# Four interleaved attention layers in one kernel: the second sliding layer's products in four column groups and its layer norms spread over the products; in the last layer, the next block's operands loaded a quad ahead and left-over projections carried on

## The chip, the cores and the metric

The kernel runs on one core of one Trainium2 chip. The metric is device time in microseconds (us), the median of several runs. The core's engines appear as in the profile: PE is TensorE (matmuls; its weight loads are listed as PEld), DVE is VectorE, ACT is ScalarE, POOL is GpSimd, SP is SyncE, on which nearly all DMAs are issued, one after the other in program order.

## What is computed

Input x is 2048 x 512 (one batch). Four layers follow each other; layers 0 and 2 use the weights A and a sliding window of 256 keys, layers 1 and 3 the weights B and all keys. Each layer is a layer norm, a projection to q, k and v of 32 heads of 16, softmax attention, a projection, and the residual.

```
def _A_ref(x, wqkv, wo):            # H = 32 heads, Dh = 16, W = 256
    q, k, v = split heads of x @ wqkv
    scores = einsum("bhqd,bhkd->bhqk", q, k) * Dh**-0.5
    mask = (i - j >= 0) & (i - j < W)
    p = softmax(where(mask, scores, -1e9))
    return heads joined of einsum("bhqk,bhkd->bhqd", p, v) @ wo
def _B_ref(...)                     # the same without the mask
x = A_x
x = x + _A_ref(_layernorm(x), A_wqkv, A_wo)    # layer 0
x = x + _B_ref(_layernorm(x), B_wqkv, B_wo)    # layer 1
x = x + _A_ref(_layernorm(x), A_wqkv, A_wo)    # layer 2
x = x + _B_ref(_layernorm(x), B_wqkv, B_wo)    # layer 3
```

## The kernel before

**Tiles.** The 2048 rows are four blocks c of 512 rows, each four tiles i of 128 rows. The 32 heads are eight quads qd of four heads. One attention step makes the scores of a quad for some keys on PE (`exps`, L745; products of 64 rows by 128 columns of the array), their exponentials on ACT (L749), and two steps later the product with v on PE (L799 in full layers, L833 in sliding ones; four groups of 32 columns, one per head; a column of ones in v gives the row sums). In a sliding layer a quad has three steps, and POOL masks the edges of each (L822, L825). In a full layer it has 16 steps. `epilogue` (L690 to L735) turns a quad's result on DVE (`ot`), divides it by the row sums and splits it into two half-precision terms (`oh`).

**Layers and loops.** Layers 0, 1 and 2 run over c and, inside, over the eight quads. Layer 3 runs over t (four pairs of quads), then c, then the two quads of t, 16 steps each. In the text steps are counted through the program: layer 1 has the steps 176 to 687, layer 3 the steps 864 to 1375. A step of a sliding layer makes two counts, so layer 2, whose block 0 has less to do, has the counts 688 to 863 in 88 steps.

**The other work** (projections K, Q, V of the next layer, the output projection `wo`, norms, transposes) is a list of `Work` generators beside the attention. `mms` (L383) issues one product as 12 matmuls (3 in O3). `PH["full"]` says that a full layer is running: then each matmul is issued as four matmuls of 32 columns (L395), otherwise as one of 128 (L398). `Side` decides after every step how much of the list goes in: `step` for sliding layers, `share` with a budget per step (its lowest value is `least`) for full ones. `finish` (L989), at the end of every block, issues all that is left of the block's list at once, apart from weight preparations.

**A layer norm.** `wo` (L659) finishes a tile of x with DVE (L672), stores it, and after the fourth tile calls `norm` (L427), which issues at once a reciprocal root of a dozen small DVE instructions and for each of the four tiles `xn` and `xh` (L448) and their difference (L454). A work T then calls `transposed` (L475) for the four tiles: a DMA transpose on SP from `xh` to `xc`, the operand of the next projections. A product with `xc` as the moving operand needs all four tiles of the block.

**Layer 3** makes the keys and queries of the next pair t+1 (K3, Q3), their maximum products (`hsum`, L562) and shifts (the store `qs<-m`, L597), the upper half of v, and the part of the output projection `wo_part` (O3) of each finished block. Blocks load their quads with `load_full` (L760 for q, L770 for k), one quad ahead inside a block, and at a block's start for its first quad.

Of the kernel before, what the change touches and what calls it, by code (L numbers as in the profile page):

```python
# [15 lines left out]
ALU = mybir.AluOpType  # L16
# [3 lines left out]
P = 128  # L20
# [169 lines left out]
def fast_path(ctx, tc, flag, a_x, a_wqkv, a_wo, b_wqkv, b_wo, out):  # L190
# [23 lines left out]
    clock, DONE, XNR, ONR = [0.0], {}, {}, {}  # L214
    LAST, STORES, EARLY = {}, [], {}

# [165 lines left out]

    def mms(ps, pairs, after=1.6, us=MM, go=True):  # L383


        if PH["full"] and pend:
            settle()
            PH["free"] = clock[0] + 1.6
            yield 0.1
        if PH["win"]:  # L390
            PH["unit"], PH["extra"] = PH["now"], 0
        for i, (a, b) in enumerate(pairs):
            if PH["full"]:
                for g in range(0, P, 32):
                    nc.tensor.matmul(ps[g:g + 32], a[:, g:g + 32], b, start=(i == 0), stop=(i == len(pairs) - 1),  # L395
                                     skip_group_check=True)
            else:
                nc.tensor.matmul(ps, a, b, start=(go and i == 0), stop=(i == len(pairs) - 1))  # L398
# [21 lines left out]
    def norm(l, c, xs, tail=False):  # L420
# [4 lines left out]
        return out  # L425

    def norm_tiles(l, c, xs, out, tail=False):  # L427

        mv = ST[l, c][1]
        y = rsqrt(nc, vp, f"{l}_{c}", mv[:, :, 1])  # L430
        if tail:
# [13 lines left out]
        for i in range(4):  # L445
            xn = vp.tile([P, D], F32, name=f"xn{l}_{c}_{i}", tag="xn", bufs=1)
            xh = vp.tile([P, 2, D], F16, name=f"xh{l}_{c}_{i}", tag="xh", bufs=XNB)
            norm1 = lambda o: nc.vector.tensor_scalar(o, xs[i], mv[:, i, 0:1], y[:, i:i + 1], op0=ALU.subtract, op1=ALU.mult)  # L448
            norm1(xn)
            if tail:  # L450
                nc.scalar.activation(xh[:, 0], xs[i], AF.Identity, bias=nb[:, i:i + 1], scale=y[:, i:i + 1])
            else:
                norm1(xh[:, 0])
            nc.vector.tensor_tensor(xh[:, 1], xn, xh[:, 0], ALU.subtract)  # L454
# [40 lines left out]

    def transpose(l, c, xns):
        for i, xh in enumerate(xns):
            yield "wait", XNR[l, c] + 2.3 * i
            transposed(l, c, i, xh)
# [159 lines left out]
    def wo(l, c, tail):  # L659

        w = weights(l % 2, 3, f"o{l}_{c}")
        xs = load_x(l, c) if tail else None
        yield wait(8)
        if not tail:
# [176 lines left out]
    class Work:  # L841
# [37 lines left out]

        done = begun = open = going = False  # L880
        proj = property(lambda self: self.name is not None and self.name[0] in ("K", "Q", "K3", "Q3"))
# [27 lines left out]
    class Side:  # L909
# [99 lines left out]
    def attention(l, works):  # L1009
# [5 lines left out]
        for t in range(NHT if l == 3 else 1):  # L1015
            for c in range(NQ):
                qds = range(2 * t, 2 * t + 2) if l == 3 else range(NQD)
                PH["spare"] = (3, 3, 2, 0)[c] if l == 2 else 0
                if l == 1:

                    sd = sd or Side(NT * NQD // 2, works[0], works[1], 0.33)
                    while ("Q", 1, c) not in DONE:
                        sd.one(True)
                    settle()
                else:
                    sd = Side((3 if win else NT) * len(qds), works[t * NQ + c], works[t * NQ + c + 1], 0.28 if l == 3 and t < 3 else 0.0)
                if win:
                    PH["run"] = RUN
                ops = loaded.pop((c, qds[0]), None) or load(l, c, qds[0])
                for qd in qds:  # L1030
                    if (l, c, qd) == (1, 0, NQD // 2):
                        sd.finish()
                        sd = Side(NT * NQD * NQ - NT * NQD // 2, works[1], works[2], 0.33)
                    nxt = None
                    if qd + 1 in qds:
                        nxt = load(l, c, qd + 1)
                    elif l < 3 and c + 1 < NQ and ("Q", l, c + 1) in DONE and (l == 1 or ("K", l, c + 1) in DONE):
                        if any(f == ("Q", l, c + 1) for _, _, f in pend):
# [4 lines left out]
                    for f in (attn_win if win else attn_full)(l, c, qd, *ops, a):  # L1043
# [4 lines left out]
                        if (l, t, c) == (3, 0, 0):  # L1048
                            sd.least = 0.28 if LOW.done else 0.5
                            while sd.k == NT - 5 and not LOW.done:  # L1050
                                sd.one(True)
                        sd.step()
                        if win and not (PH["unit"] and PH["extra"]):
# [3 lines left out]
                if l != 1 or c == NQ - 1:  # L1057
                    sd.finish()
                if not win:
# [33 lines left out]
    def shift3(ht):  # L1093
        return Work(shifted(3, ht), 0.0, None, [("K3", c, ht) for c in range(NQ)])

    def O3(c, ht):
        return Work(wo_part(c, ht), PO / 4, None, [("O", 3, c, ht)], True)

# [4 lines left out]
    def OO(l, c, tail=False):  # L1103
        return Work(later(wo, l, c, tail), PO, ("N", l + 1, c), [("O", l, c, NHT - 1), ("P", l % 2, 3)] + [("S", 0, 3)] * (l == 0 and c > 1), True)

# [95 lines left out]
    def upper(l, c, tiles=range(4)):  # L1201

        return VV(l, c, False, (1,), (), tiles)

    def side1():
        a = [Q(1, c, False) for c in (2, 3)]
# [9 lines left out]
    def side3(t, c):  # L1216
# [13 lines left out]
    works = [[side0(c) for c in range(NQ)], [[F([(qs[1, k], False) for k in (2, 3)], 16)] + [upper(1, c) for c in range(NQ)], side1()], [side2(c) for c in range(NQ)],  # L1230
             [side3(t, c) for t in range(NHT) for c in range(NQ)]]
# [63 lines left out]
```

## Time and profile before

| | |
|---|---|
| median of 3 runs | 2672.05 us (2671.59 to 2674.76) |
| the profiled execution | 2673.13 us, of it 2671.4 us span |
| granted TensorE clock | 0.997 |
| PE busy | 2591.0 us, 97% |
| ACT busy | 2384.7 us, 89% |
| DVE, POOL busy | 848.3 us (32%), 581.3 us (22%) |
| layer 0 (span) | 95 to 442 us, with its tail |
| layer 1 | 442 to 1402 us |
| layer 2, its tail | 1403 to 1657 us, 1657 to 1691.5 us |
| layer 3, the end | 1691.5 to 2656 us, 2656 to 2671.4 us |

Times in the text are counted from the start of the span. The tail of a sliding layer is the stretch after its last attention step, in which the rest of the output projection and of the next layer's first operands is made. A row of the timeline gives a run of like instructions: its start, its length, the engine, the line, what is written from what, the number of instructions, and in brackets the engine's idle time before it with what ended that. The lengths of neighbouring PE rows overlap by some 0.07 us, because matmuls are pipelined; so the price of a run is read from its start to the start of the next row.

### The profile page before, as it was taken

The page shows a single profiled execution, that of the slowest core. Times are in us where ns is not written, and L with a number is a line of the kernel's source. Part 1 is how long each engine was busy: PE and PEld are TensorE (multiplying, and loading weights), DVE is VectorE, ACT ScalarE, POOL GpSimd, SP SyncE. Part 2 cuts the span into 40 slices and gives each one's busy share as a digit, 9 for nine tenths or more (in the row PEclk, how much of TensorE's full clock was granted, in tenths as well). Part 3 has the DMA queues.
Part 4 walks back from the last instruction along what each step waited for, and adds up shares of the span by engine and source line. Part 5 has one row for each costly group of instructions (what it writes and reads, how often), then busy time and mean ns, then how long its engine had stood idle before and what let it go on. Part 6 is the DMA issues. An engine that isn't in the chain of part 4 may idle for free.

```text
span 2671.4 us, 60501 instructions
## 1 busy us (share of the span) xinstructions
PE 2591.0 (97%) x24833; PEld 762.3 (29%) x24833; DVE 848.3 (32%) x1947; ACT 2384.7 (89%) x2725; POOL 581.3 (22%) x1215
## 2 busy tenths in 40 slices
PE   8999999999999999999999999999999999999998
PEld 3333344322222222222223334422222222222221
DVE  5746653122232223111216666211111122222121
ACT  5777666999999999999997776899999999999997
POOL 1889760000000000000007787000000000000000
PEclk9999999999999999999999999999999999999999
DMA  6878785233343334222426655332222234435441
GB/s 204 210 232 252 200 226 159 69 100 112 100 103 100 100 112 111 80 68 91 132 86 193 196 154 152 115 91 80 75 68 76 72 110 146 134 113 165 144 129 49
DMA packets 293174, 341.16 MB, mean 128 GB/s; under 512 B 105928, under 2 KB 199592, under 8 KB 288280
## 3 DMA queue, kind: packets, MB, share of 16 engines
q1 hardware_dynamic: 284376, 310.17, 38.7%
q0 software_dynamic: 8512, 27.04, 3.8%
q8 instruction: 196, 3.21, 0.5%
q14 instruction: 90, 0.74, 0.1%
HBM read 226.49 MB, written 96.99 MB: 121 GB/s over the span
## 4 chain that ended last, share of the span: by engine, by line
PE 85%; ACT 5%; DVE 4%; issue 2%; DMA 1%; POOL 1%; SPq 0%; ACTq 0%; DVEq 0%
PE acc L799 34%; PE s L745 22%; PE acc L395 11%; PE b L398 10%; PE acc L833 5%; ACT e L749 5%; PE bs L398 2%; DVE ot L707 1%; POOL e L825 1%; POOL e L822 1%; DMA x<-in_A_x_dram 0%; DVE wa L330 0%; DVE sp L538 0%; PE acc L562 0%; DVE xh L454 0%
## 5 line engine op out<-in xcount | busy, mean ns | idle before, releaser
L749 ACT ACTIVATE e<-s 128x1024 f32<-128x1024 f32 (+2 forms) x2432 | 2245.9, 1115 | 136.3 <-PE s L745 121.2
L799 PE MATMUL acc<-e,vt 128*17 128x512 f32 x8192 | 1079.9, 599 | 6.9 <-DVE ot L707 6.2
L745 PE MATMUL s<-qt,kt 64*128 64x512 f16 (+3 forms) x5440 | 751.8, 355 | 27.9 <-ACT e L749 11.0
L745 PEld LDWEIGHTS <-kt 64*128 64x128 f16 x5440 | 196.0, 94 | 715.1 <-issue 694.6
L799 PEld LDWEIGHTS acc<-e,vt 128*17 128x17 f32 x8192 | 136.6, 95 | 387.9 <-issue 354.0
L825 POOL TENSOR_SCALAR_AFFINE_SELECT e<-e 128x256 f32<-128x256 f32 x512 | 230.5, 458 | 68.9 <-ACT e L749 67.9
L707 DVE STREAM_TRANSPOSE ot<-acc 128x512 f32<-128x512 f32 x128 | 91.3, 713 | 410.9 <-PE acc L799 309.3
L822 POOL TENSOR_SCALAR_AFFINE_SELECT e<-e 128x256 f32<-128x256 f32 x448 | 197.3, 446 | 46.1 <-ACT e L749 43.0
L833 PE MATMUL acc<-e,vt 128*17 128x384 f32 (+2 forms) x2816 | 197.7, 389 | 0.9 <-POOL e L825 0.5
L398 PE MATMUL b<-xc,w 128*128 128x512 f16 x664 | 159.0, 382 | 5.8 <-DVE sp L538 5.2
L651 DVE COPY vt<-acc 128x256 f32<-128x256 f32 (+1 forms) x48 | 23.6, 492 | 333.6 <-PE acc L395 333.6
L395 PE MATMUL acc<-wv,xc 128*32 128x256 f16 (+1 forms) x2304 | 121.1, 300 | 0.7 <-DVE vt L651 0.5
L537 DVE TENSOR_SCALAR sp<-acc 128x512 f16<-128x512 f32 x28 | 19.4, 692 | 294.4 <-PE acc L395 284.1
L729 POOL TENSOR_TENSOR oh<-o,oh 128x512 f16<-128x512 f32 x19 | 22.1, 1161 | 415.1 <-DVE oh L728 415.1
L656 POOL TENSOR_SCALAR vt<-vt 128x16 f32<-128x16 f32 (+1 forms) x48 | 11.1, 231 | 454.5 <-DVE vt L651 454.3
L395 PE MATMUL acc<-xc,w_h 128*32 128x512 f16 x1296 | 107.4, 379 | 2.3 <-DVE km L578 2.3
L543 POOL TENSOR_TENSOR sq<-sp 128x512 bf16<-128x512 f16 x28 | 29.1, 1039 | 369.2 <-DVE sp L537 369.2
L395 PE MATMUL acc<-xc,w 128*32 128x512 f16 x1344 | 108.9, 379 | 0.0
L543 POOL TENSOR_TENSOR sq_h<-sp_h 128x512 bf16<-128x512 f16 x27 | 28.0, 1039 | 366.4 <-DVE sp_h L537 290.5
L398 PEld LDWEIGHTS <-w 128*128 128x128 f16 x800 | 72.1, 98 | 114.9 <-issue 39.1
L395 PEld LDWEIGHTS <-xc 128*32 128x32 f16 x2304 | 65.9, 97 | 133.1 <-issue 132.7
L690 DVE SCALAR_TENSOR_TENSOR x<-acc,x 128x512 f32<-128x512 f32 x60 | 41.5, 692 | 193.8 <-PE acc L395 183.2
(163 smaller groups left out, 1684.7 us busy)
## 6 DMA issues: line engine op xcount, KB each, us to landing
kt<-kf SPq DMA_DIRECT2D x126, 512.0 KB
xd<-x SPq DMA_DIRECT2D x96, 256.0 KB
qt<-qs SPq DMA_DIRECT2D x96, 256.0 KB
x<-xd SPq DMA_DIRECT2D x96, 256.0 KB
w<-wd SPq DMA_DIRECT2D x16, 1024.0 KB
qs<-sp SPq DMA_DIRECT2D x48, 256.0 KB
wv<-wd SPq DMA_DIRECT2D x20, 512.0 KB
x<-in_A_x_dram SPq DMA_DIRECT2D x32, 256.0 KB
```

The costliest lines, as they stand in the source:

```text
L395: nc.tensor.matmul(ps[g:g + 32], a[:, g:g + 32], b, start=(i == 0), stop=(i == len(pairs) - 1), skip_group_check=True)
L398: nc.tensor.matmul(ps, a, b, start=(go and i == 0), stop=(i == len(pairs) - 1))
L543: nc.gpsimd.tensor_tensor(sq, sp[:, 0], sp[:, 0], ALU.mult)
L651: LAST["DVE"] = nc.vector.tensor_copy(to, fr).ins
L690: nc.vector.scalar_tensor_tensor(xs[i], ps, 1.0 / (UP[2] * UP[3]), xs[i], op0=ALU.mult, op1=ALU.add)
L707: nc.vector.transpose(ot.rearrange("p b r -> p (b r)"), a)
L745: nc.tensor.matmul(ps[:, h, s0:s0 + wd_], kt[R * h:R * h + R, pr, kc:kc + P], qt[R * h:R * h + R, pr, qc:qc + wd_], start=True, stop=True)
L749: LAST["ACT"] = nc.scalar.activation(e[:, :, w0:w1], ps[:, :, w0:w1], AF.Exp, scale=SCALE).ins
L799: nc.tensor.matmul(a[32 * h:32 * h + DH + 1, :], V[l, qd // 4, j // 8][:, j % 8, 4 * (qd % 4) + h, :], es_[h // 2][:, h % 2, :], start=(j ...
L822: last = nc.gpsimd.affine_select(v, v, pattern=[[0, 2], [-1, P]], compare_op=ALU.is_gt, fill=0.0, base=0, channel_multiplier=1)
L825: last = nc.gpsimd.affine_select(v, v, pattern=[[0, 2], [1, P]], compare_op=ALU.is_ge, fill=0.0, base=0, channel_multiplier=-1)
L833: nc.tensor.matmul(a[32 * h:32 * h + DH + 1, q * P:(q + nb) * P], V[l, (4 * c + j) // 4][:, j % 4, 4 * qd + h, :], es_[h // 2][:, h % 2, s ...
```

## The change

Six things are changed, all of them in what is issued and in which order; the arithmetic is the same.

1. `PH["win"]` is 2 in layer 2 (it was True), and `mms` issues each matmul there as four of 32 columns, as in a full layer. Its allowance `after` is 1.45 instead of 1.6.
2. In layer 2, and for block 1 of layer 0, `wo` hands the norm to `spread`: one tile of the norm for every finished product (counted in `READ`), with the tile's transpose issued behind it. In these stages the norm's DVE instructions are tied behind the last one of `LAST["DVE"]`.
3. In layer 2 `finish` no longer forces the transposes T, and the output projection of a block waits for the transposes of the block before.
4. In layer 1 the last part of the upper v (`LAST_UP`) may be carried over the boundary between quads 3 and 4 of block 0.
5. In layer 3 output projections O3 that are left at a block's end are carried to the next block, apart from the last block of all.
6. In layer 3 the next block's first quad is loaded a quad ahead, where its Q3 and shift are done; for t < 2 and c = 3 the upper v stands behind K3, shift and Q3, and `least` is 0.34 for c = 3.

```diff
-        PH["full"], PH["win"] = l is not None and l % 2 == 1, l is not None and l % 2 == 0
+        PH["full"], PH["win"] = l is not None and l % 2 == 1, 0 if l is None or l % 2 else max(l, 1)
-    def mms(ps, pairs, after=1.6, us=MM, go=True):
+    def mms(ps, pairs, after=1.45, us=MM, go=True):
-            if PH["full"]:
+            if PH["full"] or PH["win"] == 2:
...
+                READ.append(0)
+    def spread(l, c, xs):
+        out = []
+        for i, _ in enumerate(norm_tiles(l, c, xs, out)):
+            mark = len(READ)
+            for _ in range(5):
+                yield wait(1.2)
+                if len(READ) > mark or not PH["win"]:
+                    break
+            transposed(l, c, i, out[i])
...
+        tie = queued if PH["win"] == 2 or PH["win"] and l == 1 else lambda e: nullcontext()
...
-    def wo(l, c, tail):
-        xs = load_x(l, c) if tail else None
+        xs = load_x(l, c) if tail and l == 0 else None
...
-                XN[l + 1, c] = norm(l + 1, c, xs, tail)
+                XN[l + 1, c] = spread(l + 1, c, xs) if PH["win"] == 2 or PH["win"] and c == 1 else norm(l + 1, c, xs, tail)
...
-        def finish(self):
-            prep = lambda w: w.name is not None and w.name[0] == "P"
+        def finish(self, late=lambda w: False):
+            prep = lambda w: late(w) or w.name is not None and (w.name[0] == "P" or w.name[0] == "T" and w.aside and PH["win"] == 2)
...
-                    sd = Side(..., 0.28 if l == 3 and t < 3 else 0.0)
+                    sd = Side(..., 0.34 if l == 3 and t < 3 and c == NQ - 1 else 0.28 if l == 3 and t < 3 else 0.0)
-                        sd.finish()
+                        sd.finish(lambda w: w is LAST_UP)
+                    elif l == 3:
+                        b, u = (c + 1, t) if c + 1 < NQ else (0, t + 1)
+                        if u < NHT and ("Q3", b, u) in DONE and (b or ("H", u) in DONE):
+                            settle()
+                            loaded[b, 2 * u] = load(l, b, 2 * u)
-                    sd.finish()
+                    sd.finish(lambda w: w.out and (t, c) != (NHT - 1, NQ - 1))
...
-                a.insert(0, upper(3, h // 2, range(2 * (h % 2), 2 * (h % 2) + 2)))
+                a.insert(0 if c < 3 else len(a) - len(LATER.get((t, c), ())), upper(3, h // 2, range(2 * (h % 2), 2 * (h % 2) + 2)))
```

Three places show what moves. Line numbers of the changed kernel are some 14 to 31 higher than those of before. In the names, the numbers after `oh`, `ot` and `xh` are the block and then the quad or the tile.

On PE, in layer 2, block 1, quad 4: two half-steps' worth of products with v are followed by output projection matmuls (`b<-wo`). Before:

```order
L833 MATMUL acc_82<-e_1_3_1_1_18301,vt_1_0_0_13544 17x256 x2
L398 LDWEIGHTS oh_0_5_17674
L398 MATMUL b_18330<-wo_0_17911,oh_0_5_17674 128x512
L398 LDWEIGHTS oh_0_7_17908
L398 MATMUL b_18330<-wo_0_17911,oh_0_7_17908 128x512
```

And in the changed kernel:

```order
L853 MATMUL acc_82<-e_1_3_1_1_18775,vt_1_0_0_13544 17x256 x2
L395 LDWEIGHTS oh_0_5_17879
L395 MATMUL b_18860<-wo_0_18177,oh_0_5_17879 32x512
L395 LDWEIGHTS oh_0_5_17879
L395 MATMUL b_18860<-wo_0_18177,oh_0_5_17879 32x512
L395 LDWEIGHTS oh_0_5_17879
L395 MATMUL b_18860<-wo_0_18177,oh_0_5_17879 32x512
L395 LDWEIGHTS oh_0_5_17879
L395 MATMUL b_18860<-wo_0_18177,oh_0_5_17879 32x512
L395 LDWEIGHTS oh_0_7_18174
L395 MATMUL b_18860<-wo_0_18177,oh_0_7_18174 32x512
```

Every matmul of 128 columns has become four of 32, each with a weight load of its own. Counted over layer 2, 456 matmuls of L398 become 1824 of L395.

On DVE, at the end of layer 2: the last tile of the norm of block 2 (`xn_2_3`, `xh_2_3`) and the epilogues of the last quads of block 3 (`ot_3_5` to `oh_3_7`). Before:

```order
L448 TENSOR_SCALAR xn_2_3_20532<-x_11_20071,mv_2_20152,y_2_20503 128x512
L715 TENSOR_TENSOR op_3_4_20607<-ot_3_4_20602,r_3_4_20604 128x16x16
L454 TENSOR_TENSOR xh_2_3_20533<-xn_2_3_20532,xh_2_3_20533 128x512
L697 TENSOR_TENSOR lsum<-lsum,ot_3_4_20602 128x16
L707 STREAM_TRANSPOSE ot_3_5_20720<-acc_82 128x512
```

And in the changed kernel:

```order
L727 STREAM_TRANSPOSE ot_3_7_22272<-acc_82 128x512
L731 TENSOR_SCALAR r_3_7_22274<-ot_3_7_22272 128x16
L716 TENSOR_TENSOR lmin<-lmin,ot_3_7_22272 128x16
L717 TENSOR_TENSOR lsum<-lsum,ot_3_7_22272 128x16
L732 RECIPROCAL r_3_7_22274<-r_3_7_22274 128x16
L735 TENSOR_TENSOR op_3_6_22184<-ot_3_7_22272,r_3_7_22274 128x16x16
L741 STREAM_TRANSPOSE o_3_7_22280<-op_3_6_22184 128x512
L748 CAST oh_3_7_22282<-o_3_7_22280 128x512
L462 TENSOR_SCALAR xn_2_3_22294<-x_11_21214,mv_2_21340,y_2_21892 128x512
L749 TENSOR_TENSOR oh_3_7_22282<-o_3_7_22280,oh_3_7_22282 128x512
L462 TENSOR_SCALAR xh_2_3_22295<-x_11_21214,mv_2_21340,y_2_21892 128x512
L471 TENSOR_TENSOR xh_2_3_22295<-xn_2_3_22294,xh_2_3_22295 128x512
```

Before, the tile's last instruction stands ahead of the epilogue of quad 5; in the changed kernel it stands in the epilogue of quad 7, the last one, and behind that quad's `oh` cast.

On SP, in layer 3 at the boundary from t = 0 to t = 1: the loads of the first quads of t = 1 (`qt_0_2`, `qt_0_3`, `kt_0_2`, `kt_0_3`) and the stores ahead of them (`qs_0<-sp`, `qs_0<-m`). Before:

```order
L770 DMA kt_0_2_0_24192<-kf 128x2x1024
L770 DMA kt_0_2_1_24194<-kf 128x2x1024
L361 DMA w_0_1_h_24170<-wd_0_109 128x8x128
L551 DMA qs_0_101<-sp_0_0_h_1_24123 128x1024
L552 DMA qs_0_101<-sp_0_0_h_1_24123 128x512
L770 DMA kt_0_3_0_24198<-kf 128x2x1024
L597 DMA qs_0_101<-m_0_1_24187 8x512
L760 DMA qt_0_2_24190<-qs_0_101 128x2x512
```

And in the changed kernel:

```order
L790 DMA kt_0_2_0_25560<-kf 128x2x1024
L361 DMA wv_2_1_0_25267<-wd_2_111 128x8x256
L571 DMA qs_0_101<-sp_0_0_h_1_25220 128x1024
L572 DMA qs_0_101<-sp_0_0_h_1_25220 128x512
L617 DMA qs_0_101<-m_0_1_25242 8x512
L780 DMA qt_0_2_25558<-qs_0_101 128x2x512
L780 DMA qt_0_3_25564<-qs_0_101 128x2x512
L790 DMA kt_0_2_1_25562<-kf 128x2x1024
```

The store `qs_0<-m` and the load of q now stand ahead of the second part of k of the first quad. On PE the squares that feed that store stand at step 976 instead of step 991, the last of t = 0.

More of the change, by code (lines that the diff above doesn't have):

```diff
@@ L448, in norm_tiles @@
             norm1 = lambda o: nc.vector.tensor_scalar(o, xs[i], mv[:, i, 0:1], y[:, i:i + 1], op0=ALU.subtract, op1=ALU.mult)
-            norm1(xn)
+            with tie("DVE"):
+                norm1(xn)
             if tail:
@@ L452, in norm_tiles @@
             else:
-                norm1(xh[:, 0])
-            nc.vector.tensor_tensor(xh[:, 1], xn, xh[:, 0], ALU.subtract)
+                with tie("DVE"):
+                    norm1(xh[:, 0])
+            with tie("DVE"):
+                nc.vector.tensor_tensor(xh[:, 1], xn, xh[:, 0], ALU.subtract)
             if tail:
@@ L496, in transpose @@
     def transpose(l, c, xns):
+        if not isinstance(xns, (list, tuple)):
+            yield from xns
+            return
         for i, xh in enumerate(xns):
@@ L878, in slot @@
             return "w" if len(wused) < WB or wused[-WB].done else None
-        done = begun = open = going = False
+        done = begun = open = going = out = False
         proj = property(lambda self: self.name is not None and self.name[0] in ("K", "Q", "K3", "Q3"))
@@ L1051, in attention @@
                                 sd.one(True)
+                        while (l, c, qd) == (1, 0, NQD // 2) and sd.k == NT - 5 and not LAST_UP.done:
+                            sd.one(True)
                         sd.step()
@@ L1093, in shift3 @@
     def shift3(ht):
-        return Work(shifted(3, ht), 0.0, None, [("K3", c, ht) for c in range(NQ)])
+        return Work(shifted(3, ht), 0.0, ("H", ht), [("K3", c, ht) for c in range(NQ)])
     def O3(c, ht):
-        return Work(wo_part(c, ht), PO / 4, None, [("O", 3, c, ht)], True)
+        w = Work(wo_part(c, ht), PO / 4, None, [("O", 3, c, ht)], True)
+        w.out = True
+        return w
     def VV(l, c, act=True, halves=(0, 1), after=(), tiles=range(4)):
@@ L1103, in OO @@
     def OO(l, c, tail=False):
-        return Work(later(wo, l, c, tail), PO, ("N", l + 1, c), [("O", l, c, NHT - 1), ("P", l % 2, 3)] + [("S", 0, 3)] * (l == 0 and c > 1), True)
+        return Work(later(wo, l, c, tail), PO, ("N", l + 1, c), [("O", l, c, NHT - 1), ("P", l % 2, 3)] + [("S", 0, 3)] * (l == 0 and c > 1) + [("T", l + 1, c - 1)] * (l == 2 and c > 0), True)
     def NN(c, after=()):
@@ L1203, in upper @@
         return VV(l, c, False, (1,), (), tiles)
+    LAST_UP = upper(1, 3)
     def side1():
```

13 lines of the change are left out of this document (7 added, 6 removed).

## The prediction

> **What bounds the kernel now.** I read the page's busy shares first, then the busy time of each stage, then PE's timeline inside a step.
>
> ```profile
> PE 2591.0 (97%) x24833; PEld 762.3 (29%) x24833; DVE 848.3 (32%) x1947; ACT 2384.7 (89%) x2725; POOL 581.3 (22%) x1215
> 1403.00:1657.00 254.00, 247.57 (x2579) 94.82 (x2578) 166.72 (x409) 194.77 (x236) 200.13 (x481) 1.00 0.60 173
> 1657.00:1691.50 34.50, 32.82 (x205) 19.42 (x203) 19.44 (x48) 11.71 (x28) 0.00 (x0) 1.00 0.54 177
> 1691.50:2656.00 964.50, 942.53 (x9143) 238.47 (x9139) 174.76 (x383) 943.95 (x1024) 49.95 (x62) 1.00 0.34 103
> ```
>
> The last three rows are layer 2's steps, its tail and layer 3; their columns are the length, then PE, PEld, DVE, ACT and POOL busy. In layer 2 PE is busy for 247.57 of 254.00 us and ACT for 194.77: there only PE's own work, or a wait of PE, counts. In layer 3 PE (942.53) and ACT (943.95) are both at 98% of 964.50 us; there a gain must come from the moments in which ACT had no scores. Those are few:
>
> ```profile
>   PE s L745: 20.2, 16
> 562.97 3.77 ACT L749 ACTIVATE e<-s 128x1024 f32<-128x1024 f32 x4 [1.56 <-PE s L745]
> 1934.67 1.94 ACT L749 ACTIVATE e<-s 128x1024 f32<-128x1024 f32 x2 [4.72 <-PE s L745]
> 1937.91 1.94 ACT L749 ACTIVATE e<-s 128x1024 f32<-128x1024 f32 x2 [1.30 <-PE s L745]
> 1940.74 2.85 ACT L749 ACTIVATE e<-s 128x1024 f32<-128x1024 f32 x3 [0.89 <-PE s L745]
> 2237.56 4.71 ACT L749 ACTIVATE e<-s 128x1024 f32<-128x1024 f32 x5 [3.01 <-PE s L745]
> 2300.34 10.21 ACT L749 ACTIVATE e<-s 128x1024 f32<-128x1024 f32 x11 [3.01 <-PE s L745]
> ```
>
> The first row is layer 3's total of ACT's waits for scores: 20.2 us in 16 waits. That is the ceiling of what edits 5 and 6 can bring.
>
> **Products of 32 columns in layer 2 (edit 1).** PE's work in order of time, start and duration:
>
> ```profile
> 1498.60 0.99 PE acc L833 x16
> 1499.59 0.97 PE b L398 x4
> 1500.55 0.54 PE s L745 x8
> 1501.10 0.99 PE acc L833 x16
> 1502.09 1.83 PE b L398 x8
> ```
>
> Eight matmuls take 1.83, four 0.97: one costs (1.83 - 0.97) / 4 = 0.215, and each run of them 0.97 - 4 x 0.215 = 0.11 beyond that. Layer 3 shows what a run costs when it has the same four column groups as the product with v ahead of it:
>
> ```profile
> 2228.51 1.05 PE L799 MATMUL acc<-e,vt 128*17 128x512 f32 x8
> 2229.38 0.83 PE L395 MATMUL acc<-wo,ov 128*32 128x512 f16 x12
> 2230.14 0.61 PE L745 MATMUL s<-qt,kt 64*128 64x512 f16 x4
> 2230.68 1.05 PE L799 MATMUL acc<-e,vt 128*17 128x512 f32 x8
> 2231.66 0.60 PE L745 MATMUL s<-qt,kt 64*128 64x512 f16 x4
> ```
>
> From start to start, L799 takes 0.98 if scores follow and 0.87 if L395 follows, and twelve matmuls of L395 take 0.76. So the run adds 0.87 + 0.76 - 0.98 = 0.65, which is 3 x 0.217 and nothing beyond. Four matmuls of 32 columns thus cost what one of 128 does, and the change of the array's column split between L833 and the run falls away. The order of layer 2 has 90 runs behind L833 before; with small differences elsewhere some 95 such changes go: 90 x 0.11 = 9.9 to 95 x 0.11 = 10.5. I take **-10.5**. Nothing hides it, as PE is the bound there.
>
> In the changed order K of block 3 and K3 of block 1 begin two steps later, so two blocks start with two more steps without products. In such steps PE waits for ACT:
>
> ```profile
> 1457.27 0.40 PE L745 MATMUL s<-qt,kt 64*128 64x128 f16 x4 [1.03 <-ACT e L749]
> ```
>
> Two blocks at 0 to 1.3 each (one such wait and a small one): I take **+1.2**, bounds 0 and 2.6.
>
> **Weight loads and dispatch.** The edit adds 1368 matmuls and as many weight loads.
>
> ```profile
> L398 PEld LDWEIGHTS <-w 128*128 128x128 f16 x800 | 72.1, 98 | 114.9 <-issue 39.1
> L395 PEld LDWEIGHTS <-xc 128*32 128x32 f16 x2304 | 65.9, 97 | 133.1 <-issue 132.7
> 561.05 1.49 PE L395 MATMUL acc<-wv,xc 128*32 128x256 f16 x48 [0.52 <-DVE vt L651]
> ```
>
> A weight load of 32 columns takes 97 ns. If PE made them one after the other, four would take 0.39 where the product has 0.216; but 48 matmuls with their loads went by in 1.49 us, 31 ns each. So neither sets the pace in a run of this length. The changed step has 8 + 16 + 16 = 40 matmuls in 2.39 us, 60 ns each, or 56 in 3.25, for hundreds of us on end; before it was 28 in 2.50, 89 ns. No row shows 60 ns sustained, so the price lies between 0 and the rival below; I take 0, by the nearest row.
>
> [...]
>
> **The norm at the end of layer 2 (edits 2 and 3).** Here the change adds a wait. The tail's first product, K3 of block 2, has `xc` of block 2 as its operand and needs all four tiles.
>
> ```profile
> 1656.09 1.04 PE L833 MATMUL acc<-e,vt 128*17 128x384 f32 x12 [0.25 <-POOL e L822]
> 1657.07 2.76 PE L398 MATMUL bs<-xc,w_h 128*128 128x512 f16 x12
> 1660.20 2.10 PE L398 MATMUL b<-wo,oh 128*128 128x512 f16 x9 [0.36 <-DMA wo<-wd]
> 1647.54 1.58 SPq L475 DMA_TRANSPOSE xc<-xh  x1
> 1657.18 0.72 DVE L707 STREAM_TRANSPOSE ot<-acc 128x512 f32<-128x512 f32 x1 [3.21 <-PE acc L833]
> 1660.16 0.69 DVE L729 TENSOR_TENSOR oh<-o,oh 128x512 f16<-128x512 f32 x1
> 1641.34 0.62 DVE L448 TENSOR_SCALAR xh<-x,mv,y 128x512 f16<-128x512 f32 x1
> 1641.88 0.88 DVE L454 TENSOR_TENSOR xh<-xn,xh 128x512 f16<-128x512 f32 x1
> 1931.21 2.62 DMA qt<-qs
> ```
>
> Before, the last transpose was issued at 1647.54, ten us before K3 began. In the changed order the last tile's `xn`, `xh` and difference stand on DVE behind the last quad's `ot`, which waits for the last L833, and SP has the transpose behind that. What is queued behind them on DVE and SP is the tail's own work. Counted from the old times: `ot` at 1657.18 to the `oh` cast's end at 1660.16; then `xn` (0.54), the `oh` difference (0.61), `xh` (0.54), the difference (0.88): 1662.7. The transpose's landing has no row; the issue row's 1.58 and the 2.62 of the load of q bound it from below and above, and I take the latter: 1665.4. PE then stands for 1665.4 - 1657.1 = 8.3 us, less the 0.36 for `wo`, whose transfer is then done. And a long pause has a second price, which layer 0 shows:
>
> ```profile
> 289.97 1.86 PE L398 MATMUL b<-xc,w 128*128 128x512 f16 x4 [4.50 <-DVE sp L538]
> 291.76 1.04 PE L745 MATMUL s<-qt,kt 64*128 64x256 f16 x8
> 292.73 1.91 PE L833 MATMUL acc<-e,vt 128*17 128x384 f32 x16
> 302.69 2.76 PE L398 MATMUL b<-xc,w 128*128 128x512 f16 x12
> ```
>
> After 4.50 us of pause the first three run at half pace: 1.86, 1.04 and 1.91 where the normal rows have 1.04, 0.61 and 1.06, a loss of 2.1. So the tail gets 8.3 - 0.36 + 2.1 = **+10**. Bounds: 0, if the last tile's work still runs ahead, and +12.
>
> **Layer 0 (edit 2).** The pause above came from DVE, which worked off the whole norm of block 1 before the `sp` that PE waited for. Spread, the norm no longer stands there, and 4.50 + 2.1 = 6.6 us go. But K of layer 1's block 1 now needs the last tile's transpose, and in the order that tile's work comes behind more of the attention's. K began at 302.69; without the 6.6, and one more step (1.5 without products) later, PE would be ready for it at about 297.5. The order's DVE rows with the durations above put the last tile's difference, an estimate, at 298 to 300, and its transpose 2.62 later, so that 3.1 to 5.1 come back, and above some 4 the half pace too. I take **-1**, bounds -6.6 and +3.
>
> **Layer 1 (edit 4).** The row at 562.97 is the burst of 14 products at step 239, which the changed order spreads over steps 240 to 244, two or three each: **-1.5**.
>
> **Layer 3 (edits 5 and 6).** At the boundary 1934.67 the first scores of t = 1 waited for squares, `qs<-m` and q in a chain. In the changed order the squares are issued 15 steps earlier and the loads follow at once, so the chain ends before the boundary: 4.72 + 1.30 + 0.89 = 6.9 go, the last two being the half pace after the pause. The two waits of 3.01 belong to blocks of t = 2 whose end held nine forced matmul groups:
>
> ```profile
> 2234.68 0.83 PE L395 MATMUL acc<-wo,ov 128*32 128x512 f16 x12 [0.79 <-DVE x L690]
> 2236.31 0.83 PE L395 MATMUL acc<-wo,ov 128*32 128x512 f16 x12 [0.79 <-DVE x L690]
> ```
>
> Each tile of O3 waited 0.79 for DVE to empty the only bank, with no scores in between. Carried on, these go one or two matmul groups a step, and the waits fall beside the attention. That is 6.0, and some 2 of the smaller waits of t = 2; the rest of the 20.2 stays, since PE has about as much to do there as ACT. Together **-15**, bounds -8 (only the boundary and a little) and -18.
>
> **The sum.** -1 - 1.5 - 10.5 + 1.2 + 10 - 15 = -16.8. From the profiled execution, 2673.13, that is 2656.3. The median before lies 1.1 below it, so I put the median after at about **2656**.
>
> **The rivals.**
>
> *No pause at the end of layer 2.* DVE's scheduled order is read from the program, so this needs K3 to be ready by another path. Layer 0's new wait may fall away too. Either gives 2640 to 2647. For it: ten us of slack before. Against it: the order shows the tile behind `ot`. Chance 0.14.
>
> *PE's rate of matmuls is the limit.* If a sustained step goes no faster than the 63 ns of the row at 2229.38 (0.76 / 12), a step of 40 takes 2.52 and one of 56 takes 3.53, against 2.50 and 3.36 before. The 456 matmuls in 90 runs are 66 runs of four and 24 of eight, if there are no others, so that is +1.3 + 4.1 = 5.4 in place of -10.5: 2672, no change. For it: no sustained row below 89 ns. Against it: the burst at 31. Chance 0.12. [...]
>
> *The loads of layer 2 stand behind the transposes: slower.* Each spread transpose waits on SP, in order, for its tile's DVE work, and q and k of the next quads are queued behind it; it also holds SP for 1.58 us itself. PE would stop at a quad's first scores. By layer 0's rows such a stop is 4.5 + 2.1 = 6.6. The gains without it are 16.8, so from three stops on nothing is left, and five of the twelve tiles make it 2656 + 33 = 2689. For it: the change ties these DVE instructions behind others. Against it: before, the same transposes stood between the same loads, which are issued a quad, some 7.5 us, ahead. Chance 0.12.
>
> **How the numbers follow.** The forecast has 0.62, with a range of its own of 2649 to 2667 by the bounds of the tail, layer 0 and layer 3; 0.14, 0.12 and 0.12 go to the rivals. The likeliest case gives 2656. The range of 8 in 10 reaches from 2643, inside the first rival, to 2673, past the second; it leaves out the third and the best of the first. About 0.2%, 5.3 us, is what a measurement of this kernel can tell from no change. Faster by more than that, below 2666.7: the forecast, whose own range ends there, and the first rival, 0.76. Within 0.2%: the second rival, 0.12. Slower: the third, 0.12.
>
> **What would show it.** Step by step in the changed profile: products of layer 2 in steps of about 2.39 and 3.25, not 2.50 and 3.36; PE's pause of 6 to 9 us ahead of K3 in the tail, ended by `xc`, with a drop of the granted clock behind it; no pause of 4.50 at 289.97 but one ahead of K of layer 1's block 1; no wait of ACT at the boundary to t = 1, and less than 8 us of its waits left in layer 3. The prediction is wrong if PE waits for q or k inside layer 2, if L395 runs there take over 0.23 per product, or if carrying the projections on makes new waits in the next blocks.

## The result, and the profile after

The changed kernel takes 2655.18 us (median of 4 runs, 2654.4 to 2656.71), the kernel before 2671.82 us in the runs beside it; the ratio is 0.9938, with a 95% interval of 0.9921 to 0.9955. The forecast was 2656. Its span is 2653.0 us, 18.4 less than before, and this is where the difference arises. The stages are those of one profiled run of each kernel. A stage is taken from a row that both profiles have: the first exponential of layer 1, layer 2's first scores of 384 columns, the start of the last quad's `ot`, layer 3's first exponential and the end of its last one.

| stage | before, us | after, us | difference | forecast |
|---|---|---|---|---|
| to the end of layer 0 | 443.07 | 442.40 | -0.7 | -1 |
| layer 1 | 959.17 | 955.25 | -3.9 | -1.5 |
| layer 2 | 254.94 | 246.47 | -8.5 | -9.3 |
| its tail | 34.60 | 44.56 | +10.0 | +10 |
| layer 3 | 964.23 | 949.35 | -14.9 | -15 |
| the end | 15.39 | 14.97 | -0.4 | 0 |

The busy times by stage, in the changed kernel (length, then PE, PEld, DVE, ACT, POOL, the granted clock, the DMA engines' share, GB/s), answer to the rows of before: layer 2, PE's pause at its end, the rest of the tail, layer 3.

```profile
1398.00:1644.00 246.00, 238.54 (x3949) 110.26 (x3947) 166.28 (x406) 194.88 (x236) 200.57 (x481) 1.00 0.61 174
1644.00:1653.00 9.00, 0.07 (x2) 0.02 (x1) 5.01 (x12) 0.00 (x0) 0.00 (x0) 0.59 0.82 229
1653.00:1688.50 35.50, 34.10 (x203) 19.81 (x205) 16.02 (x39) 11.72 (x28) 0.00 (x0) 0.96 0.47 147
1688.50:2638.00 949.50, 937.08 (x9143) 234.29 (x9138) 174.75 (x383) 944.27 (x1024) 50.06 (x62) 1.00 0.35 105
```

In layer 2 PE has nine us less to do. In the second row it does nothing for nine, and the granted clock falls to 0.59. In layer 3 ACT is busy as long as before, in 15 us less.

The chain of work inside layer 2 after (start, duration, what) has the new step:

```profile
1485.82 1.73 PE b L395 x32
1487.54 0.54 PE s L765 x8
1488.08 0.99 PE acc L853 x16
...
1492.33 0.86 PE b L395 x16
```

Thirty-two matmuls of 32 columns take 1.73 where eight of 128 took 1.83, sixteen take 0.86 where four took 0.97.

PE's and DVE's timelines, then SP's, then a piece of the chain, at the end of layer 2 after:

```profile
1643.03 1.04 PE L853 MATMUL acc<-e,vt 128*17 128x384 f32 x12 [0.25 <-POOL e L842]
1653.01 4.17 PE L398 MATMUL bs<-xc,w_h 128*128 128x512 f16 x12 [8.94 <-DMA xc<-xh]
1657.02 2.75 PE L398 MATMUL b<-wo,oh 128*128 128x512 f16 x12
```

```profile
1644.12 0.72 DVE L727 STREAM_TRANSPOSE ot<-acc 128x512 f32<-128x512 f32 x1 [2.49 <-PE acc L853]
...
1646.98 0.54 DVE L462 TENSOR_SCALAR xn<-x,mv,y 128x512 f32<-128x512 f32 x1
...
1648.61 0.69 DVE L471 TENSOR_TENSOR xh<-xn,xh 128x512 f16<-128x512 f32 x1
```

```profile
1649.33 1.26 SPq L492 DMA_TRANSPOSE xc<-xh  x1
```

```profile
1649.33 3.43 DMA xc<-xh
```

PE's pause ahead of K3 is 8.94 us and ends with the transpose; K3 takes 4.17 instead of 2.76. From `ot` to the tile's last instruction DVE needs 5.2 us, and the transpose lands 3.43 after its issue.

In layer 0, PE's pause at 289.97 is gone, and K of block 1 waits for its last transpose instead. It begins at 302.82, where it began at 302.69 before:

```profile
302.82 2.75 PE L398 MATMUL b<-xc,w 128*128 128x512 f16 x12 [2.94 <-DMA xc<-xh]
```

In layer 3, ACT's waits for scores, in total, and its run over the boundary to t = 1:

```profile
  PE s L765: 4.9, 8
```

```profile
1899.86 220.51 ACT L769 ACTIVATE e<-s 128x1024 f32<-128x1024 f32 x240 [0.24 <-PE s L765]
```

From 20.2 us in 16 waits, 4.9 in 8 are left, and 240 exponentials run across the boundary without a wait.

### The profile page after: what moved, and what is told of

It reads as the page before. It is cut to its first block, busy times and chain, and to the rows that moved or that the text cites. A ratio compares the mean times of both kernels' runs of the same rounds, so it can differ in the third digit from the quotient of the medians.

```text
span 2653.0 us, 63247 instructions
## 1 busy us (share of the span) xinstructions
PE 2574.1 (97%) x26201; PEld 771.2 (29%) x26201; DVE 850.7 (32%) x1947; ACT 2385.5 (90%) x2725; POOL 583.9 (22%) x1215
## 4 chain that ended last, share of the span: by engine, by line
PE 85%; ACT 6%; DVE 4%; issue 3%; DMA 1%; POOL 1%; ACTq 0%; SPq 0%; DVEq 0%
PE acc L819 34%; PE s L765 22%; PE acc L395 11%; PE b L398 7%; ACT e L769 5%; PE acc L853 5%; PE b L395 3%; PE bs L398 2%; DVE ot L727 1%; DMA x<-in_A_x_dram 0%; POOL e L845 0%; POOL e L842 0%; DVE xh L471 0%; DVE xh L462 0%; DVE sp L558 0%
## 5 line engine op out<-in xcount | busy, mean ns | idle before, releaser
L765 PEld LDWEIGHTS <-kt 64*128 64x128 f16 x5440 | 190.2, 94 | 697.8 <-issue 680.3
L853 PE MATMUL acc<-e,vt 128*17 128x384 f32 (+2 forms) x2816 | 195.8, 387 | 0.6 <-POOL e L842 0.5
L398 PE MATMUL b<-xc,w 128*128 128x512 f16 x520 | 122.5, 380 | 5.7 <-DMA xc<-xh 2.9
L395 PE MATMUL acc<-wv,xc 128*32 128x256 f16 (+1 forms) x2304 | 120.7, 299 | 0.2 <-DVE km L598 0.2
L395 PEld LDWEIGHTS <-xc 128*32 128x32 f16 x2688 | 77.1, 97 | 137.7 <-issue 132.8
L395 PE MATMUL acc<-xc,w_h 128*32 128x512 f16 x1296 | 105.7, 379 | 2.3 <-DVE km L598 2.3
L395 PE MATMUL acc<-xc,w 128*32 128x512 f16 x1344 | 108.0, 379 | 0.0
L557 DVE TENSOR_SCALAR sp_h<-acc 128x512 f16<-128x512 f32 x27 | 18.5, 686 | 227.1 <-PE acc L395 227.1
```

Source lines behind the costliest of these rows:

```text
L557: nc.vector.tensor_scalar(sp[:, 0], ps, e, None, op0=ALU.mult)
L765: nc.tensor.matmul(ps[:, h, s0:s0 + wd_], kt[R * h:R * h + R, pr, kc:kc + P], qt[R * h:R * h + R, pr, qc:qc + wd_], start=True, stop=True)
L853: nc.tensor.matmul(a[32 * h:32 * h + DH + 1, q * P:(q + nb) * P], V[l, (4 * c + j) // 4][:, j % 4, 4 * qd + h, :], es_[h // 2][:, h % 2, s ...
```

## The experiments

All stage times below are taken as in the table, each from one profiled run. Where only one run was timed, the text says so.

### Columns: alone, taken back, and with twice the matmuls

`only_32` is the kernel before with the one edit:

```diff
-        PH["full"], PH["win"] = l is not None and l % 2 == 1, l is not None and l % 2 == 0
+        PH["full"], PH["win"] = l is not None and l % 2 == 1, 0 if l is None or l % 2 else max(l, 1)
-            if PH["full"]:
+            if PH["full"] or PH["win"] == 2:
                 for g in range(0, P, 32):
```

> The kernel before with one edit alone: layer 2's matmuls of 128 columns as four of 32. Theory (change of the array's column split costs 0.11 us per run, 90 to 95 runs): layer 2's steps take 243.5 us instead of 253.9, the whole 10.5 us less than before. Rival (rate of matmuls at 63 ns): layer 2 5 us longer than before. Second rival (weight loads one after the other at 97 ns): 0.39 instead of 0.216 per product, 456 of them, 78 us longer.

Measured: 2664.41 us, ratio 0.9976 (0.9965 to 0.9987). Layer 2 takes 248.79 us, 6.15 less than before, neither the 10.5 of the theory nor the loss of either rival. Busy times of layer 2 in this kernel and, for comparison, in the kernel before over the same stage:

```profile
1403.12:1651.91 248.79, 239.72 (x3956) 110.87 (x3953) 169.31 (x409) 194.76 (x236) 201.31 (x481) 1.00 0.63 178
```

```profile
1402.24:1657.18 254.94, 248.51 (x2588) 95.25 (x2585) 167.34 (x409) 195.08 (x236) 200.13 (x481) 1.00 0.60 173
```

PE's work falls from 248.51 to 239.72, by 8.8 us, 0.098 for each of the 90 runs of products; but its pauses grow from 6.4 to 9.1 us (stretch less busy time). Two of them, on PE's timeline:

```profile
1484.60 0.40 PE L562 MATMUL b<-sq,hsum 128*32 128x512 bf16 x4 [0.77 <-DVE x L672]
1513.36 1.05 PE L395 MATMUL b<-xc,w 128*32 128x512 f16 x16 [0.97 <-DVE sp L538]
```

The first was 0.36 before, and stands behind an epilogue on DVE; the second is new, and `sp` stands there behind a norm in one piece. So the price of a run was nearly right, and a part of it turns into waits, mostly for DVE.

`no_32` is the changed kernel with this edit taken back:

```diff
-            if PH["full"] or PH["win"] == 2:
+            if PH["full"]:
```

> The changed kernel with layer 2's matmuls back at 128 columns; the order of the products stays. Theory: 0.11 us for each of some 90 runs come back: 10 us more than the changed kernel, layer 2's steps 255.5 us instead of 245.4. Rival: most of layer 2's gain came from the spread norms and not from the columns: less than 4 us more.

Measured: 2667.87 us, ratio 0.9985 (0.9976 to 0.9995); layer 2 takes 255.66 us, 9.2 more than in the changed kernel. With the rest of the change the columns are worth 9.2, alone 6.15: the other 3 us belong to both together. Without the columns the rest of the change brings layer 2 nothing (255.66 against 254.94 before).

What a run pays can be seen on PE and its weight loads (PEld), behind L833 in the kernel before and behind L853 in the changed one:

```profile
1502.01 0.55 PEld L398 LDWEIGHTS <-oh 128*128 128x128 f16 x4 [0.64 <-issue]
1502.02 1.04 PE L398 MATMUL b<-wo,oh 128*128 128x512 f16 x4
```

```profile
1488.68 1.63 PEld L395 LDWEIGHTS <-oh 128*32 128x32 f16 x32
1488.89 1.91 PE L395 MATMUL b<-wo,oh 128*32 128x512 f16 x32
```

With 32 columns the first load runs 0.21 us ahead, beside the matmuls with v; with 128 it starts only with its own matmul. Over all such runs of layer 2 (medians) the first matmul starts 312 ns after the last one with v in `no_32` (311 in the kernel before), and 196 ns in the changed kernel. The difference, 116 ns, is the price of a run, and it is about the length of one weight load, 97 to 98 ns. Whether the late load is all of it is not shown.

`half_moving` doubles the number of matmuls:

```diff
+                    if PH["win"] == 2:
+                        m = b.shape[-1] // 2
+                        for z in range(2):
+                            nc.tensor.matmul(ps[g:g + 32, z * m:(z + 1) * m], a[:, g:g + 32], b[:, z * m:(z + 1) * m],
+                                             start=(i == 0), stop=(i == len(pairs) - 1), skip_group_check=True)
+                        continue
```

> The changed kernel with each matmul of 32 columns in layer 2 done as two over half of the moving columns: twice the matmuls and weight loads, the same columns in all. Theory (pace set by moving columns, nothing by the number of matmuls): 2 x 0.110 per product by the 256-wide rows of layer 1, layer 2 within 3 us of the changed kernel. [...]

It does not compute the projections of layer 2 rightly, so only its time (one run) is read. Layer 2 takes 248.17 us, 1.7 more than the changed kernel. Its chain (L398 is here the line of the halves):

```profile
1484.77 1.75 PE b L398 x64
1486.52 0.54 PE s L771 x8
1487.06 0.99 PE acc L859 x16
...
1494.61 0.87 PE b L398 x32
```

Sixty-four matmuls with their weight loads take 1.75, and a step of 88 takes 3.28: 37 ns each, in step after step of layer 2. So at the changed kernel's 60 ns the rate of matmuls sets nothing, and the prediction's rival of a limit at 63 ns has fallen.

### The tail

`tail_norm` makes the norm of layer 2's block 2 at once again:

```diff
-                XN[l + 1, c] = spread(l + 1, c, xs) if PH["win"] == 2 or PH["win"] and c == 1 else norm(l + 1, c, xs, tail)
+                XN[l + 1, c] = spread(l + 1, c, xs) if PH["win"] == 2 and c != 2 or PH["win"] and l == 0 and c == 1 else norm(l + 1, c, xs, tail)
```

> The changed kernel with the norm of layer 2's block 2 issued at once instead of spread; all else of the change stays. Theory: the tail's pause (8.94 us ahead of K3) and K3's half pace (1.4) go, the wait for wo of 0.36 comes back: some 10 us less, 2645 us, first scores of layer 3 some 35.7 us after the start of the last L853 instead of 45.7. Rival: the norm's DVE burst then holds up PE inside block 3, as it did in layer 0 before (4.5 and 2.1 us of half pace): only 3 to 4 us less, 2651 us.

Measured: 2654.11 us, ratio 0.9932 (0.9916 to 0.9949), hardly less than the changed kernel. PE's timeline at the end of layer 2:

```profile
1639.66 1.29 PE L395 MATMUL b<-wv,xc 128*32 128x256 f16 x32 [2.40 <-DVE km L598]
1651.05 2.76 PE L398 MATMUL bs<-xc,w_h 128*128 128x512 f16 x12
1656.12 4.04 PE L398 MATMUL b<-wo,oh 128*128 128x512 f16 x12 [2.30 <-DMA wo<-wd]
```

K3 follows without a pause: the late tile was the tail's cause, as forecast. But the tail shrinks by 6.3 only (38.26), since the load of `wo` is late now, 2.30 with half pace behind it (4.04 for 2.75), and layer 2 grows by 2.3 because DVE makes the maximum of the keys (`km`) behind the norm's burst. Layer 0, which the edit leaves as it is, was 4 us longer in this profile; 3.1 of them stand at one place, at 367.95, where K waits 3.24 for `sp` and takes 4.03, while in the changed kernel it waits 1.40 and takes 2.75. Both theory and rival were half right.

`tq_wo` keeps the spread, but lets block 2's wait at most once for a finished product, and opens `wo` earlier:

```diff
-            for _ in range(5):
+            for _ in range(1 if (l, c) == (3, 2) else 5):
                 yield wait(1.2)
...
             if l:
+                for wk in tails[l]:
+                    if wk.w and not wk.open and wk.may_open():
+                        wk.advance()
                 ahead(1, 0, "3_0_0_h0", 0)
```

> The changed kernel with the spread of block 2 in layer 2 waiting at most once 1.2 us for a finished product, instead of five times, and wo of the tail opened ahead of the two early weight loads. In the order the last tile's xh then stands ahead of ot of quad 6 and the maximum of the keys ahead of all tiles but the first. Theory: the tail's pause of 8.94 goes and what norm at once brought (2.40 inside block 3) does not come: layer 2 246.5, the tail 36 to 38 where the changed kernel has 44.6, 2647 us. Rival: DVE has no room for the tile inside block 3, so PE waits there for 2 us or more: 2650 us.

Measured: 2650.12 us, ratio 0.9916 (0.9899 to 0.9932). Layer 2 takes 247.26 and the tail 36.66, 7.9 less than in the changed kernel. In its tail:

```profile
1647.27 2.75 PE L398 MATMUL bs<-xc,w_h 128*128 128x512 f16 x12 [1.23 <-issue]
1651.15 2.75 PE L398 MATMUL b<-wo,oh 128*128 128x512 f16 x12 [1.13 <-DMA wo<-wd]
```

Two waits of some 1.2 are left, and the products behind them run at full pace. The rival's wait of 2 us inside block 3 did not come. The median lies below both kernels; its interval still touches that of the changed kernel, so what is shown is the tail, not the size of the gain to a us. The two edits were not taken apart.

### Layer 0

`l0_1` makes the spread of layer 0's block 1 wait at most once as well, on top of `tq_wo`:

```diff
-            for _ in range(1 if (l, c) == (3, 2) else 5):
+            for _ in range(1 if (l, c) == (3, 2) else 1 if l == 1 else 5):
```

> As tq_wo, and the spread of block 1 in layer 0 waits at most once as well, which puts its last tile ahead of the next product's sp. Theory: the wait of 2.94 us for the last transpose in layer 0, with or without half pace behind it, shrinks to under 1 us: 2 to 4 us less than tq_wo. Rival: the old wait for sp comes back in part (DVE works off the norm at once again), no gain against tq_wo.

Measured: 2649.94 us, ratio 0.9914 (0.9897 to 0.9930), no gain against `tq_wo`. The theory fell. The rival has the size right, but not the cause: PE now waits once, for 6.06, and the profile puts the end of that wait down to a store on SP's queue. What K really waited for there stays open.

```profile
300.99 5.01 PE L398 MATMUL b<-xc,w 128*128 128x512 f16 x12 [6.06 <-DMA kf<-sp]
```

`best32` makes layer 0's products 32 columns wide as well:

```diff
-            if PH["full"] or PH["win"] == 2:
+            if PH["full"] or PH["win"]:
```

> As l0_1, and layer 0's products inside the attention as four of 32 columns too. Theory: as in layer 2, 0.11 us for each of some 80 runs, 8 to 9 us less than l0_1. Rival: layer 0 has DVE and POOL work close behind PE, so that half of it turns into waits, as with the columns alone in layer 2 (6.2 of 9.2): 3 to 5 us less.

Measured: 2654.93 us, ratio 0.9929 (0.9912 to 0.9946). Layer 0 ends at 446.15, later than in `l0_1` (442.82). Both expectations were wrong here. On PE's timeline:

```profile
225.07 3.44 PE L395 MATMUL b<-xc,w 128*32 128x512 f16 x32 [5.56 <-DVE sp L558]
303.28 4.45 PE L395 MATMUL b<-xc,w 128*32 128x512 f16 x48 [3.77 <-DMA xc<-xh]
339.84 0.50 PE L765 MATMUL s<-qt,kt 64*128 64x256 f16 x5 [2.23 <-issue]
```

From 95 us to its end PE's work in layer 0 falls by 4.4 us against `l0_1` (330.90 for 335.27), and its pauses grow by 7.7 (20.2 for 12.5). The longest, of 5.56, is new: on DVE `sp` stands there behind the norm of block 0, which is not spread, and half pace follows (3.44 where 1.91 is usual). So layer 0 shows what the columns cost where a norm stands in one piece. What held the wait of 2.23 stays open.

### Layers 1 and 3: which edit does what

`no_last_up` takes edit 4 back:

```diff
-                        sd.finish(lambda w: w is LAST_UP)
+                        sd.finish()
...
-                        while (l, c, qd) == (1, 0, NQD // 2) and sd.k == NT - 5 and not LAST_UP.done:
-                            sd.one(True)
```

> The changed kernel without edit 4: the last part of the upper v is issued at once at the boundary of quads 3 and 4. The burst of 14 products comes back there, 1.5 us; if the carried part is also the cause of the rest, layer 1 takes 955.25 + 3.9; if the rest comes from the allowance of mms, 955.25 + 1.5.

One run: layer 1 takes 958.41, 3.2 more than the changed kernel. ACT's waits are back at the boundary and behind it:

```profile
564.79 35.35 ACT L769 ACTIVATE e<-s 128x1024 f32<-128x1024 f32 x38 [1.82 <-PE s L765]
600.68 26.03 ACT L769 ACTIVATE e<-s 128x1024 f32<-128x1024 f32 x28 [0.54 <-PE s L765]
627.11 33.39 ACT L769 ACTIVATE e<-s 128x1024 f32<-128x1024 f32 x36 [0.40 <-PE s L765]
661.50 173.18 ACT L769 ACTIVATE e<-s 128x1024 f32<-128x1024 f32 x188 [1.00 <-PE s L765]
```

`after_16` takes only the allowance back:

```diff
-    def mms(ps, pairs, after=1.45, us=MM, go=True):
+    def mms(ps, pairs, after=1.6, us=MM, go=True):
```

> The changed kernel with the allowance of mms back at 1.6. Layer 1 gained 3.9 us where 1.5 were forecast. If the shorter allowance, which lets the next product begin sooner after the last, is the cause, layer 1 takes 955.25 + 1.5 to 2.5 us; if the carried upper v is the cause, it stays within 0.3 us of 955.25.

One run: layer 1 takes 954.35, 0.9 less, not more. So the allowance is not the cause in layer 1; the carried upper v is, for 3.2 of the 3.9. The remaining 0.7 stays open.

`no_ahead` takes edit 6 back:

```diff
-                        if u < NHT and ("Q3", b, u) in DONE and (b or ("H", u) in DONE):
+                        if False:
-                ... 0.34 if l == 3 and t < 3 and c == NQ - 1 else 0.28 ...
+                ... 0.28 ...
-                a.insert(0 if c < 3 else len(a) - len(LATER.get((t, c), ())), upper(...))
+                a.insert(0, upper(...))
```

> The changed kernel without edit 6: in layer 3 no loads a quad ahead over a block's end, the upper v again ahead of K3, shift and Q3, least 0.28 in block 3. Theory: the chain of squares, store of the maxima and load of q at the boundary to t = 1 comes back with the half pace behind it, layer 3 takes 949.4 + 6 to 8 us. Rival: the carried projections of edit 5 alone had made room for it, under 2 us.

One run: layer 3 takes 955.59, 6.2 more. The boundary's wait is back, and behind it the 1.30 that came with half pace in the kernel before (there the granted clock was 0.52 from 1933.9 to 1940 us):

```profile
1930.28 1.94 ACT L769 ACTIVATE e<-s 128x1024 f32<-128x1024 f32 x2 [4.84 <-PE s L765]
1933.51 1.94 ACT L769 ACTIVATE e<-s 128x1024 f32<-128x1024 f32 x2 [1.30 <-PE s L765]
```

Which of the three parts of edit 6 does it was not tried.

`no_carry` takes edit 5 back:

```diff
-                    sd.finish(lambda w: w.out and (t, c) != (NHT - 1, NQ - 1))
+                    sd.finish()
```

> The changed kernel without edit 5: output projections of layer 3 left at a block's end are issued at once again. Theory: the waits of 3.01 us at two block ends of t = 2 come back with smaller ones, layer 3 takes 949.4 + 6 to 9 us. Rival: PE has as much to do in t = 2 as ACT, so the work only moves and layer 3 changes by less than 2 us.

One run: layer 3 takes 949.37, as in the changed kernel. The theory fell, but not for the rival's reason: in this kernel's order nothing is left to burst. A group is four matmuls of 32 columns. The last eight steps of the first of the two blocks of t = 2 held 1, 0, 2, 1, 0, 3, 0, 9 groups before, and hold 1, 2, 1, 2, 1, 2, 1, 3 in this kernel; with an allowance of 1.45 the next product may begin a step sooner, so the list is through at the block's end. Undoing this alone (`after_16`) left layer 3 at 949.71, because the carry then takes the rest over. So both were undone:

```diff
-    def mms(ps, pairs, after=1.45, us=MM, go=True):
+    def mms(ps, pairs, after=1.6, us=MM, go=True):
-                    sd.finish(lambda w: w.out and (t, c) != (NHT - 1, NQ - 1))
+                    sd.finish()
```

> The changed kernel without edit 5 and with the allowance of mms back at 1.6. Undone alone, neither moved layer 3. In the order of this kernel the nine matmul groups stand at the ends of two blocks of t = 2 again. Theory (either of the two edits is enough to spread them): the two waits of 3.01 us come back, layer 3 takes 949.4 + 6 us or a little more. Rival (the groups no longer wait for DVE, for another reason): layer 3 within 2 us of 949.4.

One run: layer 3 takes 954.58, 5.2 more, with the waits back at both places:

```profile
2231.07 31.70 ACT L769 ACTIVATE e<-s 128x1024 f32<-128x1024 f32 x34 [3.01 <-PE s L765]
2263.10 27.73 ACT L769 ACTIVATE e<-s 128x1024 f32<-128x1024 f32 x30 [0.34 <-PE s L765]
2293.84 75.37 ACT L769 ACTIVATE e<-s 128x1024 f32<-128x1024 f32 x82 [3.01 <-PE s L765]
```

Either edit is enough. `no_ahead` and this run together account for 11.4 of layer 3's 14.9 us; no run shows what the other 3.5 come from.

## Why the prediction was right, and where it was not

**Columns in layer 2** (-10.5 forecast). The price of 0.11 per run held: taking the edit back cost 9.2, which is 0.107 for each of the 86 runs behind L853 in the changed order. The size was a us too large, since the sum took 95 runs. "Nothing hides it" was wrong for the edit alone: there PE's work fell by 8.8, and 2.6 of it came back as pauses. The rival of the rate of matmuls, with a chance of 0.12, is refuted at 37 ns each. The rival of the loads behind the transposes fell too: PE's only wait for a load in layer 2 of the changed kernel is one of 0.07 us.

**Steps without products** (+1.2). PE's pauses in layer 2 were 6.4 us before (254.94 less 248.51) and are 7.5 after (246.00 less 238.54): +1.1. The steps without products are there, but they brought only one new wait for ACT, of 0.52; the rest is small waits of other kinds. So the total of this term was right in part by luck.

**The tail** (+10). 8.94 of pause where 8.3 stood in the sum, 1.4 of half pace where 2.1 did, and no wait for `wo`: +10.0. That these errors cancel is luck. The transpose's landing was taken as 2.62 from a load of q and took 3.43. The rival without a pause has fallen. That the pause comes from the late tile is shown by `tail_norm` and `tq_wo`, where K3 follows at once or after 1.23.

**Layer 0** (-1). The pause moved from `sp` to the last transpose, 2.94 for 4.50, as said. PE was ready for K at 299.88 (302.82 less 2.94) and not at 297.5, because it waited four times for ACT just ahead, 0.5 to 0.7 us each, which the sum did not have. That half pace comes only above some 4 us of pause was an estimate from the one row with 4.50, and did not hold in other runs (last section). The total of -0.7 is one profile's, and the other runs put it anywhere between -3 and +4, so that it agrees with the forecast is luck.

**Layer 1** (-1.5). The mechanism was right and the size was not: the burst's own wait was counted, but not the waits of 0.52, 0.20 and 1.00 behind it, which go with it. The term measured 3.2 by `no_last_up`.

**Layer 3** (-15). The total held at 14.9. The boundary's 6.9 measured 6.2, and the two waits of 3.01, put at 6.0, measured 5.2; 3.5 are left where the sum had some 2. For the two waits of 3.01 the step named the wrong owner: it gave them to the carry alone, and the runs show that the allowance of 1.45, which the forecast passed over as a part of edit 1, does the same. It took the run with both undone to see either.

## What to carry to other kernels

A run of matmuls with 128 columns behind matmuls of 32 columns cost 0.11 us here beyond its matmuls, whether it had four or eight of them, so products that alternate in small runs may as well use the same split. But what that saves can come back as waits where another engine's work stands in one piece: a part of it in layer 2 with the norms as they were, and more than all of it in layer 0. Work that is spread must be finished before the last place where something else stands ahead of it: one tile behind the last epilogue took back 10 of 28 us. And a part that has no effect when it is undone alone may still be a cause, if another part covers for it.

## What the runs showed of the hardware

Half pace came after much shorter pauses of PE than the 4.50 us of the profile before, and not always. The twelve matmuls of K in layer 0 (2.75 at full pace) and the pauses ahead of them, in `tail_norm`, `tq_wo`, `half_moving` and `no_32`; the changed kernel's own row above has 2.94 of pause and full pace. For the first two, a row of products with v from a few us earlier is shown ahead of it (1.06 at full pace):

```profile
296.02 1.91 PE L853 MATMUL acc<-e,vt 128*17 128x384 f32 x16
...
302.15 4.44 PE L398 MATMUL b<-xc,w 128*128 128x512 f16 x12 [2.26 <-DVE r L731]
```

```profile
294.75 1.77 PE L853 MATMUL acc<-e,vt 128*17 128x384 f32 x16
...
301.09 4.44 PE L398 MATMUL b<-xc,w 128*128 128x512 f16 x12 [2.17 <-DVE r L731]
```

```profile
300.78 5.28 PE L404 MATMUL b<-xc,w 128*128 128x512 f16 x12 [2.95 <-DVE r L737]
```

```profile
302.80 4.12 PE L398 MATMUL b<-xc,w 128*128 128x512 f16 x12 [3.21 <-DVE lsum L717]
```

Pauses of 2.94 and 2.95 went once without and once with it, with shorter pauses just ahead in both: four of 0.5 to 0.7 in the changed kernel, and some 2.4 us in all from 290 us on in `half_moving`. In `tail_norm` and `tq_wo` half pace had come already before the pause of 2.2, in the products with v, and there only three pauses of 0.74, 0.54 and 0.52 us stood ahead of it; the granted clock was 0.83 in the stretch from 290 to 300 us of `tq_wo`. So half pace followed a row of short pauses here, as it followed one long pause elsewhere, and in some runs only: the changed kernel has pauses of 0.73, 0.54 and 0.52 at the same place, with full pace behind them (1.06 for the products with v) and a granted clock of 1.00 from 290 to 300 us. What decides between the two is not shown. Half pace is a part of why layer 0 varies by some us from run to run (K alone took 1.4 to 2.5 us longer in the four rows above), and hence differences of a few us between these kernels are read from the stage concerned and not from one total.
